# One set of transposes for the value and the one-hot columns of the gate, and the table's products one slot later

## The chip, the cores and the metric

The kernel runs on one core of a Trainium2 chip, in one launch. The metric is the device time in microseconds (us) from the start to the end of one execution. Engines: PE is TensorE (matrix products and transposes), PEld its weight loads, DVE VectorE, ACT ScalarE, POOL GpSimd, SP SyncE, which issues most DMAs.

## The reference

Causal attention over 8 batches of 12 heads, 448 tokens each, and behind it a mixture of 8 experts that takes at most 80 tokens per expert, the 80 with the largest gate weight over all 3584 tokens. In short:

```python
scores = where(causal, q @ k.T / 8, -1e9);  attn = softmax(scores);  x = attn @ v     # 8 x 12 x 448 x 64
logits = x @ w_gate;  e = argmax(logits);  p = softmax(logits)[e]                      # 3584 tokens, 8 experts
for each expert e: tok = tokens of e, at most capacity = 80, those with the largest p
    out[tok] = p[tok] * (relu(x[tok] @ w1[e]) @ w2[e])                                 # other rows are 0
```

## The kernel before

**Attention.** Heads are worked two at a time, 6 pairs to a batch, 48 pairs. A pair takes 8 slots. In slots 0 to 6 PE makes a tile of scores `sp` (L423, L424, the last one L433 to L436) from float16 halves of q and k (`qk`), DVE adds the mask, scales and takes the minimum (`ns`, L445), and ACT takes the exponent (`prob`, L448). In slots 0, 2, 4 and 6 PE also transposes four blocks of the pair before (`tp`, L465), which ACT copies to `PT` (L477). In slot 7 the products with v follow (`xp`, L495), which DVE copies out (L500). Two pairs are one "third" of a batch: while one third is worked, the next one's q and k are split in high and low halves, by casts (POOL L384 twice, DVE L387 twice) and subtractions (POOL L390, L391, L395).

**The gate.** When a batch's attention is done, its gate weights, the choice of an expert for each token and the rank of each token within its expert are worked out in the slots of the two batches that follow. `goh` is the one-hot of the chosen expert, `gow` the same times the gate weight `ggw`. `columns` (L698) and `parts` (L709) write with POOL, per 128 tokens, five groups of 8 columns to `mv` (two for the token's place, L703 and L705, three bfloat16 parts of the weight, L713 to L716) and three copies of the one-hot to `oh` (L702). `expert_rows(i)` (L723) turns them by PE: four transposes of `oh` (i=0) and four of the last three groups of `mv` (i=1) into a bank `selt` each (L731), of which DVE copies 24 rows to `ex[:, 0]` and `ex[:, 1]` (L734). With `ex` PE then makes the comparisons: `rl` (L761, the batch against the table of the 80 best so far), `rn` (L745, the batch against itself), which DVE reduces (`lt` L767, `less` L748); `cp` (L774) and `ro` (L779) give the table's new ranks.

**The table.** Some 30 slots later `rr` (L849, two halves) is the one-hot of the tokens' ranks, and `tn` (L859: 8 products with the old table `tab`, absent in the first batch; L862: 4 products with `mv`) gathers the 80 best in PSUM. DVE copies them to `tab` (L873), PE turns that (`rp`, L877) and DVE copies `row` (L881), which the next batch's `rl` needs.

**What sets the order.** It is written out by hand. The tables `STEPS` (batches 0 to 5) and `EARLY` (batch 6) give each step a slot counted from the end of its batch; in a slot the steps stand behind the slot's score group, in slot 6 of a pair between its transposes and the last score group. The last batch has a list of its own (`TAIL`). Each engine works its instructions in the order in which they are written. A step of slot 80 of one batch meets slot 32 of the next, both in the fifth pair of a batch. Small PSUM banks (`selt`, `rl`, `rn`, `cp`, `tn`, `rp`, `gt`, `rt`) share two buffers in turn.

In the sections below, "the third gate" is that of the third batch; it is worked, with the second batch's table, in the fourth batch's fifth pair, which starts at 150.46 us of the trace. The code:

Of the kernel before, what the change touches and what calls it, by code (L numbers as in the profile page):

```python
# [10 lines left out]
BF16 = mybir.dt.bfloat16  # L11
# [6 lines left out]
P = 128  # L18
# [34 lines left out]
def attention_then_moe(  # L53
# [19 lines left out]
    NT = (S + P - 1) // P  # L73
# [24 lines left out]
    def bank(shape, dtype, name):  # L98
        return (ps_x or ps_m).tile(shape, dtype, name=name, tag="x" if ps_x else "misc")
# [20 lines left out]
    NV = 5  # L120
# [11 lines left out]
    for r in range(2):  # L132
        t = akeep.tile([P, OFF_L + NT * P], F32, name=f"prob{r}")
# [7 lines left out]
    for r in range(2):  # L141
        t = akeep.tile([P, NT, PH * P], F32, name=f"vt{r}")
# [74 lines left out]
    mv = one_hots = mv_flat = oh_flat = expert_cols = tables = table_rows = None  # L217
    identb = before = dec = number = number_after = pnum = tbase = wgd = slots_e = slots_t = None
# [32 lines left out]
    def late_constants():  # L251


        def padded(shape, name):
            t = spool.tile(shape, BF16, name=name, tag=name, bufs=1)
            nc.gpsimd.memset(t, 0.0)
            return t
# [21 lines left out]
        def slots():  # L279
            nonlocal mv_flat, mv, slots_e, slots_t  # L280
            many = max(1, NSL)
            slots_e = const.tile([SL, many, E, SL], COUNT, name="slots_e")
            slots_t = const.tile([P, many, NT, SL], COUNT, name="slots_t")
            for t, k in ((slots_e, E), (slots_t, NT)):
                nc.gpsimd.iota(t, [[SL, many], [0, k], [1, SL]], base=0, channel_multiplier=0,
                               allow_small_or_imprecise_dtypes=True)
            mv_flat = padded([P, (NT - 1) * NV * E + 2 * E + P], "mv")
            mv = mv_flat[:, 0:NT * NV * E].rearrange("k (t v e) -> k t v e", v=NV, e=E)

        def operands():  # L290
            nonlocal oh_flat, one_hots, expert_cols, tables, table_rows
# [399 lines left out]
    def select_groups(bt):  # L691

        b = bt.b
        last = b == B - 1
# [147 lines left out]
        def move(s):  # L842
# [43 lines left out]
            if not last and NSL == 1:  # L886
# [549 lines left out]
```

## Time and profile before

| | |
|---|---|
| median of 3 runs | 467.88 us (467.48 to 468.62) |
| profiled execution | 467.61 us |
| its span in the trace | 465.7 us |
| PE busy over the span | 441.2 us (95%) |
| PEld, DVE, ACT, POOL busy | 346.3 (74%), 414.5 (89%), 392.3 (84%), 309.1 (66%) us |
| granted PE clock | 1.00 |

The span is what the trace shows from the first instruction to the last; the execution's own time is 1.9 us more. Busy shares are averages over attention (to about 318 us) and the experts behind it. A row of a timeline gives start, duration, engine, line and operation, out<-in, the tile's shape and a count; instructions of one kind in a row are drawn together. A bracket at its end is idle time of the engine just before, with what ended it. PE works several instructions at once, so its rows overlap; the distance of starts is what an instruction costs PE.

### The profile page before, as it was taken

What the parts mean: (1) busy time and instruction counts of PE and PEld (TensorE: products, weight loads), DVE (VectorE), ACT (ScalarE), POOL (GpSimd) and SP (SyncE); (2) the same over time, 40 slices, a digit from 0 to 9 for tenths busy, and PEclk for the clock granted to TensorE, in tenths of its full rate; (3) what the DMA queues carried; (4) which work ended last, traced back from release to release, by engine and by line L of the source; (5) the groups of instructions that cost most, each with busy time, mean ns of one, the idle gap of its engine ahead of it and who ended that gap; (6) DMA issues with size and microseconds to landing.
All of it is one profiled execution on the core that took longest, in us unless ns stands there. A gap on an engine that the chain in (4) does not pass through costs nothing.

```text
span 465.7 us, 14169 instructions
## 1 busy us (share of the span) xinstructions
PE 441.2 (95%) x4973; PEld 346.3 (74%) x4973; DVE 414.5 (89%) x1286; ACT 392.3 (84%) x1077; POOL 309.1 (66%) x382
## 2 busy tenths in 40 slices
PE   4998999999999999999999999999989999999994
PEld 1676666866777786677777767776558999999993
DVE  6888889988998999899899989989589999999792
ACT  6997989878988997898889789888587998988791
POOL 7999999988987987898798789760153133310001
PEclk9999999999999999999999999999999999999999
DMA  8658899989769578966957987439948999999931
GB/s 217 182 158 236 230 304 275 271 242 306 206 209 297 171 232 253 270 184 211 298 163 223 279 243 220 161 129 344 410 157 274 397 391 391 398 425 423 423 132 44
DMA packets 42998, 120.84 MB, mean 260 GB/s; under 512 B 6146, under 2 KB 23810, under 8 KB 39472
## 3 DMA queue, kind: packets, MB, share of 16 engines
q1 hardware_dynamic: 41712, 116.21, 76.8%
q0 software_dynamic: 1056, 3.51, 2.4%
q8 instruction: 39, 0.64, 0.6%
q10 hardware_dynamic: 160, 0.23, 0.2%
q14 instruction: 31, 0.25, 0.2%
HBM read 96.36 MB, written 23.99 MB: 258 GB/s over the span
## 4 chain that ended last, share of the span: by engine, by line
PE 75%; DVE 9%; POOL 5%; DMA 4%; issue 3%; ACT 2%; SPq 1%; POOLq 0%; DVEq 0%; ACTq 0%
PE xp L495 15%; PE tp L465 15%; PE sp L423 6%; PE sp L424 5%; PE rt L592 4%; PE hp L1231 3%; PE op L1231 3%; PE op L1239 3%; PE sp L433 3%; PE gp L545 3%; PE hp L1246 3%; PE hp L1245 3%; PE hp L1243 2%; DMA qk<-k_t 2%; DVE wl L1165 2%
## 5 line engine op out<-in xcount | busy, mean ns | idle before, releaser
L448 ACT ACTIVATE prob<-ns,nb 128x128 f32<-128x128 f32 (+3 forms) x336 | 177.1, 529 | 23.0 <-DVE nb L445 20.6
L445 DVE CUSTOM_DVE_ANT_0 ns<-sp,mask 128x384 f32<-128x384 f32 (+2 forms) x288 | 116.2, 413 | 20.2 <-PE sp L424 16.5
L465 PE MATMUL tp<-ident,prob 128*128 128x128 f32 x768 | 118.4, 277 | 1.1 <-ACT prob L448 0.9
L477 ACT COPY PT<-tp 128x512 f32<-128x512 f32 x182 | 104.1, 573 | 17.8 <-PE sp L423 8.4
L395 POOL TENSOR_TENSOR qk<-qk,qk 128x448 f16<-128x448 f32 x92 | 95.8, 1063 | 13.1 <-DVE qk L387 7.4
L465 PEld LDWEIGHTS tp<-ident,prob 128*128 128x128 f32 x768 | 89.8, 142 | 12.1 <-ACT PT L477 2.5
L1165 DVE SCALAR_TENSOR_TENSOR wl<-wraw,wh 128x768 f16<-128x768 f32 (+1 forms) x91 | 92.5, 1081 | 3.2 <-ACT wh L1180 3.2
L495 PE MATMUL xp<-PT,vt 128*64 128x448 f32 (+3 forms) x768 | 91.1, 380 | 0.0
L495 PEld LDWEIGHTS xp<-PT,vt 128*64 128x64 f32 x768 | 53.8, 137 | 42.7 <-issue 22.7
L423 PE MATMUL sp<-qk 128*128 128x384 f16 (+2 forms) x288 | 75.9, 279 | 8.2 <-ACT qk L355 5.2
L1180 ACT ACTIVATE wh<-wraw 128x768 f16<-128x768 f32 (+1 forms) x91 | 79.0, 931 | 3.6 <-PE hp L1246 1.8
L424 PE MATMUL sp<-qk 128*128 128x384 f16 (+2 forms) x288 | 78.3, 278 | 1.3 <-DVE qk L349 0.8
L448 ACT ACTIVATION_READ_ACCUMULATOR prob<-ns,nb 128x1 f32 x336 | 64.0, 190 | 0.0
L1332 POOL DMA_INDIRECT out<-yo,idx x8 | 14.7, 1832 | 70.8 <-ACT yo L1329 66.6
L390 POOL TENSOR_TENSOR qk<-qk,qk 64x448 f16<-64x448 f32 x46 | 54.8, 1190 | 3.4
L391 POOL TENSOR_TENSOR qk<-qk,qk 64x448 f16<-64x448 f32 x46 | 51.0, 1109 | 3.2
L423 PEld LDWEIGHTS <-qk 128*128 128x128 f16 x288 | 28.5, 99 | 17.3 <-issue 8.0
L387 DVE CAST qk<-qk 128x896 f16<-128x896 f32 x46 | 40.4, 879 | 0.1
L384 POOL CAST qk<-qk 64x896 f16<-64x896 f32 x40 | 37.4, 935 | 4.4 <-PE sp L436 3.2
L1246 PEld LDWEIGHTS <-wl 128*128 128x128 f16 x362 | 36.1, 100 | 0.9 <-DVE wl L1165 0.7
L1243 PEld LDWEIGHTS <-wh 128*128 128x128 f16 x362 | 36.4, 101 | 0.0
L1245 PEld LDWEIGHTS <-wh 128*128 128x128 f16 x362 | 36.2, 100 | 0.0
(192 smaller groups left out, 927.7 us busy)
## 6 DMA issues: line engine op xcount, KB each, us to landing
wraw<-w SPq DMA_DIRECT2D x27, 1536.0 KB, 15.7
qk<-k_t SPq DMA_DIRECT2D x92, 224.0 KB, 5.5
out<-mask_l SPq DMA_DIRECT2D x56, 192.0 KB, 4.6
qk<-q_t SPq DMA_DIRECT2D x23, 448.0 KB, 4.2
vt<-v_t SPq DMA_DIRECT2D x24, 384.0 KB, 5.7
xs<-xr SPq DMA_DIRECT2D x42, 192.0 KB, 2.9
wraw<-w SPq DMA_DIRECT2D x24, 256.0 KB, 5.9
vt<-v_t SPq DMA_DIRECT2D x24, 64.0 KB, 5.3
```

What stands on the lines that cost most here:

```text
L390: nc.gpsimd.tensor_tensor(out=qa[hi, i], in0=qf[lo, i], in1=qa[lo, i], op=ALU.subtract)
L391: nc.gpsimd.tensor_tensor(out=qb[lo, i], in0=qf[hi, i], in1=qb[hi, i], op=ALU.subtract)
L395: nc.gpsimd.tensor_tensor(out=k_lo[j][:, i], in0=kf[j][:, i], in1=k_hi[j][:, i], op=ALU.subtract)
L423: nc.tensor.matmul(sp[:, 0:w], qx[:, p, t * P:w], kx[:, p, 0:w], start=True, stop=False)
L424: nc.tensor.matmul(sp[:, 0:w], qx[:, p, t * P:w], lx[:, p, 0:w], start=False, stop=True)
L445: pr.masked = nc.vector.tensor_tensor_reduce(out=ns[:, 0:w], in0=sp[:, 0:w], in1=m, scale=-1.0 / 8.0, scalar=HUGE, op0=ALU.add, op1=ALU.mi ...
L448: nc.scalar.activation(pr.P[:, off:off + w], ns[:, 0:w], AF.Exp, bias=nb, scale=-1.0, accum_out=total)
L465: nc.tensor.transpose(pr.tp[:, i], pr.P[:, off:off + P], ident)
L477: copy(dst, src)
L495: state["pe"] = nc.tensor.matmul(xp[rows, 0:w], st["vt"][:, c, p * P + j * DH:p * P + (j + 1) * DH], pr.PT[:, j, n0:n0 + w], start=(c == 0 ...
L1165: return nc.vector.scalar_tensor_tensor(out=l, in0=src, scalar=SW, in1=h, op0=ALU.mult, op1=ALU.subtract)
L1180: nc.scalar.activation(h, src, AF.Copy, scale=SW)
```

## The change

For the first seven batches the one-hot copies move into `mv`. Per 128 tokens `mv` gets 16 groups of 8 columns (128 columns) in place of 5; the values stand in groups 2 to 6, the three one-hot copies in groups 8 to 10, the rest stays zero from the one memset at the start, which grows from 264 to 544 columns. One set of four transposes (`both_rows`) turns all of it into one bank; the two copies take rows 64 to 87 (`ex[:, 0]`) and rows 32 to 55 (`ex[:, 1]`) of that bank. The last batch keeps its two sets, with its copies by ACT. 28 transposes, their 28 weight loads and seven banks go. In the tables, `parts` goes from slot 33 to 32, the transposes stand in slot 33 (before: 32 and 34), the copies in 34 and 35, and `tn`, `tab`, `rp` and `row` go from 77, 78, 80, 81 to 78, 79, 81, 82. In `EARLY` only the transposes and copies move.

```diff
-STEPS = {... 'parts': 33, 'r0t': 32, 'r0c': 33, 'r1t': 34, 'r1c': 35, 'rl': 36, ... 'rr': 73, 'tn': 77, 'tab': 78, 'rp': 80, 'row': 81, 'rr_more': 75}
-EARLY = {... 'parts': 32, 'r0t': 33, 'r0c': 33, 'r1t': 34, 'r1c': 34, 'rl': 35, ...}
+STEPS = {... 'parts': 32, 'r1t': 33, 'r0c': 34, 'rl': 36, 'lt': 36, 'r1c': 35, ... 'rr': 73, 'tn': 78, 'tab': 79, 'rp': 81, 'row': 82, 'rr_more': 75}
+EARLY = {... 'parts': 32, 'r1t': 33, 'r0c': 34, 'r1c': 35, 'rl': 35, ...}
...
-            mv_flat = padded([P, (NT - 1) * NV * E + 2 * E + P], "mv")
-            mv = mv_flat[:, 0:NT * NV * E].rearrange("k (t v e) -> k t v e", v=NV, e=E)
+            mv_flat = padded([P, NT * P + 4 * E], "mv")
+            mv = mv_flat[:, 0:NT * P].rearrange("k (t v e) -> k t v e", t=NT, e=E)
...
-            m, oh3 = bt.m, bt.oh3 = mv, one_hots
+            m = bt.m = mv[:, :, 2:2 + NV, :]
+            oh3 = bt.oh3 = one_hots if last else mv[:, :, 8:11, :]
...
-                (nc.scalar.copy if last else nc.vector.tensor_copy)(bt.ex[0:3 * E, i], got[0][0:3 * E])
+                nc.scalar.copy(bt.ex[0:3 * E, i], got[0][0:3 * E])
             return [turn, copy]
+
+        def both_rows():
+            got = []
+
+            def turn():
+                selt = bank([P, NT * P], BF16, "selt")
+                got.append(selt)
+                for t in range(NT):
+                    nc.tensor.transpose(selt[:, t * P:(t + 1) * P], mv_flat[:, t * P:(t + 1) * P], identb)
+
+            def copy(i):
+                r = 4 * E if i else 8 * E
+                nc.vector.tensor_copy(bt.ex[0:3 * E, i], got[0][r:r + 3 * E])
+            return [turn, lambda: copy(0), lambda: copy(1)]
...
-        r0, r1 = expert_rows(0), expert_rows(1)
+        rows = [f for i in range(2) for f in expert_rows(i)] if last else both_rows()
```

Three places show the new order. On PE, at the first batch's table (from the second batch on, eight more `tn` products with `tab` stand ahead of these four), before:

```order
L424 MATMUL sp<-qk_1_115 128x384
L862 LDWEIGHTS rr
L862 MATMUL tn<-mv,rr 80x40
L862 LDWEIGHTS rr
L862 MATMUL tn<-mv,rr 80x40
L862 LDWEIGHTS rr [waits DVE_49]
L862 MATMUL tn<-mv,rr 80x40
L862 LDWEIGHTS rr
L862 MATMUL tn<-mv,rr 80x40
L465 MATMUL tp<-ident,prob_104 128x128 [waits Activation_49]
L465 MATMUL tp<-ident,prob_104 128x128 x3
L433 LDWEIGHTS qk_1_115
```

and now (L862 of before is L877):

```order
L424 MATMUL sp<-qk_1_115 128x384
L465 MATMUL tp<-ident,prob_104 128x128 [waits Activation_49]
L465 MATMUL tp<-ident,prob_104 128x128 x3
L877 LDWEIGHTS rr
L877 MATMUL tn<-mv,rr 80x40
L877 LDWEIGHTS rr
L877 MATMUL tn<-mv,rr 80x40
L877 LDWEIGHTS rr [waits DVE_49]
L877 MATMUL tn<-mv,rr 80x40
L877 LDWEIGHTS rr
L877 MATMUL tn<-mv,rr 80x40
L433 LDWEIGHTS qk_1_115
```

The fourth group of attention transposes has moved ahead of the table's products.

On PE, around the transposes of the third gate, before the second set stands behind a group of attention transposes:

```order
L465 MATMUL tp<-ident,prob_106 128x128 [waits Activation_49]
L465 MATMUL tp<-ident,prob_106 128x128 x3
L731 LDWEIGHTS mv [waits DVE_49,Pool_49]
L731 MATMUL selt<-identb,mv 128x128 [waits PE_49]
L731 LDWEIGHTS mv
```

and now the only set stands one score group earlier than that, behind the second score tile of the pair and the turned table `rp`:

```order
L424 LDWEIGHTS qk_1_115
L424 MATMUL sp<-qk_1_115 128x128 [waits Pool_49]
L892 LDWEIGHTS tab_1_680 [waits DVE_49]
L892 MATMUL rp_2761<-identb,tab_1_680 128x80
L745 LDWEIGHTS mv [waits Pool_49]
L745 MATMUL selt<-identb,mv 128x128 [waits PE_49]
```

The first set, which stood ahead of that score tile, is gone.

On DVE, in the fifth pair of a batch from its second score tile on (`ns` 128x128 to 128x384 are the masks of its tiles, CAST the two casts of the next third's k), before:

```order
L445 ISA ns,nb<-sp,mask 128x128 [waits PE_49,Activation_49]
L445 ISA nb 128x1
L881 COPY row_0_682<-rp_1977 24x80
L734 COPY ex<-selt 24x512
L387 CAST qk_1_115<-qk_113 128x896 [waits DMAHW1_49,DMAHW0_49]
L445 ISA ns,nb<-sp,mask 128x256 [waits PE_49,Activation_49]
L445 ISA nb 128x1
L445 ISA ns,nb<-sp,mask 128x256 [waits PE_49,Activation_49]
L445 ISA nb 128x1
L734 COPY ex<-selt 24x512
L387 CAST qk_1_115<-qk_113 128x896 [waits DMAHW3_49,DMAHW2_49]
L445 ISA ns,nb<-sp,mask 128x384 [waits PE_49,Activation_49]
```

and now:

```order
L445 ISA ns,nb<-sp,mask 128x128 [waits PE_49,Activation_49]
L445 ISA nb 128x1
L387 CAST qk_1_115<-qk_113 128x896 [waits DMAHW1_49,DMAHW0_49]
L445 ISA ns,nb<-sp,mask 128x256 [waits PE_49,Activation_49]
L445 ISA nb 128x1
L896 COPY row_0_682<-rp_1984 24x80
L749 COPY ex<-selt 24x512
L445 ISA ns,nb<-sp,mask 128x256 [waits PE_49,Activation_49]
L445 ISA nb 128x1
L749 COPY ex<-selt 24x512
L387 CAST qk_1_115<-qk_113 128x896 [waits DMAHW3_49,DMAHW2_49]
L445 ISA ns,nb<-sp,mask 128x384 [waits PE_49,Activation_49]
```

The `row` copy and the first `ex` copy have moved behind the first cast and one mask; the cast stands where they stood. The order on POOL and SP is the same as before.

## Rows read from the trace of the kernel before

**Rows 1.** Busy time of the engines in a stretch of one batch's length: start:end, length, then busy us (instructions) of PE, PEld, DVE, ACT and POOL, the granted PE clock, DMA share, GB/s.

```profile
143.97:184.33 40.36, 39.92 (x372) 29.27 (x372) 37.59 (x143) 35.31 (x113) 34.61 (x44) 1.00 0.78 230
```

**Rows 2.** All waits of PE from 66 to 310 us, the six batches in which the gates run: what waited for what, us in total, times, longest.

```profile
PE tn L862 <- DVE rr L849: 1.9, 5, 0.6
PE tp L465 <- ACT prob L448: 0.5, 1, 0.5
PE rt L592 <- DVE gfm L652: 0.3, 1, 0.3
PE sp L423 <- DVE nb L445: 0.3, 1, 0.3
```

**Rows 3.** PE's timeline around the second batch's table products, a pair ahead of the third gate's transposes.

```profile
146.71 0.45 PE L859 MATMUL tn<-tab,rm 80*80 80x5 bf16 x8
147.01 0.23 PE L862 MATMUL tn<-mv,rr 128*80 128x40 bf16 x2
147.57 0.25 PE L862 MATMUL tn<-mv,rr 128*80 128x40 bf16 x2 [0.32 <-DVE rr L849]
147.66 0.64 PE L465 MATMUL tp<-ident,prob 128*128 128x128 f32 x4
148.23 0.38 PE L433 MATMUL sp<-qk 128*64 128x448 f16 x1
```

**Rows 4.** DVE's timeline at the same place.

```profile
147.20 0.32 DVE L849 TENSOR_TENSOR rr<-rank,slots_t 128x160 bf16<-128x160 f16 x1
```

**Rows 5.** ACT's timeline at the same place: the copy that empties the bank which the fourth group of attention transposes takes.

```profile
145.99 0.57 ACT L477 COPY PT<-tp 128x512 f32<-128x512 f32 x1
```

**Rows 6.** PE's timeline around the two sets of transposes of the third gate.

```profile
151.06 0.39 PE L731 MATMUL selt<-identb,oh 128*128 128x128 bf16 x4
...
151.62 0.60 PE L465 MATMUL tp<-ident,prob 128*128 128x128 f32 x4
152.25 0.38 PE L731 MATMUL selt<-identb,mv 128*128 128x128 bf16 x4
152.47 0.27 PE L423 MATMUL sp<-qk 128*128 128x256 f16 x1
```

**Rows 7.** DVE's timeline in the same pair.

```profile
151.93 0.18 DVE L881 COPY row<-rp 24x80 bf16<-24x80 bf16 x1
152.04 0.40 DVE L734 COPY ex<-selt 24x512 bf16<-24x512 bf16 x1
152.37 0.60 DVE L387 CAST qk<-qk 128x896 f16<-128x896 f32 x1
...
153.59 0.41 DVE L734 COPY ex<-selt 24x512 bf16<-24x512 bf16 x1
153.92 0.60 DVE L387 CAST qk<-qk 128x896 f16<-128x896 f32 x1
154.45 0.54 DVE L445 CUSTOM_DVE_ANT_0 ns<-sp,mask 128x384 f32<-128x384 f32 x1
```

**Rows 8.** POOL's timeline in the same pair: the second cast of q and the first subtraction.

```profile
151.39 0.93 POOL L384 CAST qk<-qk 64x896 f16<-64x896 f32 x1
152.40 1.48 POOL L390 TENSOR_TENSOR qk<-qk,qk 64x448 f16<-64x448 f32 x1
```

**Rows 9.** DVE's timeline in the second batch: one of its casts beside POOL's cast of the next rows.

```profile
59.91 1.34 DVE L387 CAST qk<-qk 128x896 f16<-128x896 f32 x1
```

**Rows 10.** POOL's timeline there.

```profile
59.83 0.93 POOL L384 CAST qk<-qk 64x896 f16<-64x896 f32 x1
```

**Rows 11.** DVE's timeline in the first gate's pair: the second cast, beside POOL's subtraction of the next rows.

```profile
73.62 0.60 DVE L387 CAST qk<-qk 128x896 f16<-128x896 f32 x1
```

**Rows 12.** POOL's timeline there.

```profile
73.54 1.58 POOL L390 TENSOR_TENSOR qk<-qk,qk 64x448 f16<-64x448 f32 x1
```

**Rows 13.** POOL's timeline at a place where no cast of DVE meets the subtraction.

```profile
78.42 1.03 POOL L390 TENSOR_TENSOR qk<-qk,qk 64x448 f16<-64x448 f32 x1
```

**Rows 14.** DVE's timeline in the pair behind the third gate's: what empties the two small PSUM banks.

```profile
156.84 0.73 DVE L748 SCALAR_TENSOR_TENSOR less<-rn,ggw,before 128x512 bf16<-128x512 f32 x1
...
158.46 0.21 DVE L779 TENSOR_SCALAR ro<-cp,pnum 80x8 f16<-80x8 f32 x1
```

**Rows 15.** PE's timeline there: the comparison that takes the bank which `ro` empties.

```profile
158.75 0.27 PE L745 MATMUL rn<-ex 128*128 128x256 bf16 x1
```

**Rows 16.** PE's timeline in the first gate's pair: the first set of transposes, the score tile behind the second set, the one behind that, and the first comparison.

```profile
70.44 0.39 PE L731 MATMUL selt<-identb,oh 128*128 128x128 bf16 x4
...
71.66 0.27 PE L423 MATMUL sp<-qk 128*128 128x256 f16 x1
...
73.07 0.32 PE L423 MATMUL sp<-qk 128*128 128x384 f16 x1 [0.27 <-DVE nb L445]
...
73.83 0.38 PE L745 MATMUL rn<-ex 128*128 128x512 bf16 x1
```

**Rows 17.** POOL's timeline there: the last write to `mv` ahead of the transposes.

```profile
71.08 0.24 POOL L716 TENSOR_TENSOR mv<-grest,mv 128x32 bf16<-128x32 f32 x1
```

**Rows 18.** PE's timeline in the last batch's attention, behind the table products of the sixth batch: transposes of rows (`rt`), and the last score group.

```profile
309.87 0.52 PE L592 MATMUL rt<-ident,xu 128*128 128x128 f32 x3 [0.31 <-DVE gfm L652]
...
310.76 0.38 PE L433 MATMUL sp<-qk 128*64 128x448 f16 x1
```

**Rows 19.** The memset of `mv` in the view of its line: duration in ns, start in us, shape.

```profile
L256 POOL MEMSET mv<- x1: 309/309/309, 36.9 to 36.9; 128x264 bf16 x1
```

More of the change, by code (lines that the diff above doesn't have):

```diff
@@ L32 @@
 ROWS1 = [59, 62, 64, 65]
-STEPS = {'gp': 18, 'gs': 18, 'lp': 21, 'lg': 22, 'logit': 23, 'shifted': 25, 'chosen': 26, 'sums': 27, 'one_hot': 28, 'weight': 28, 'weighted': 31, 'columns': 30, 'parts': 33, 'r0t': 32, 'r0c': 33, 'r1t': 34, 'r1c': 35, 'rl': 36, 'lt': 36, 'c3w': 38, 'c3l': 39, 'cp': 40, 'ro': 41, 'c2w': 41, 'c2l': 43, 'c1w': 43, 'c1l': 44, 'c0w': 46, 'c0l': 46, 'gt': 47, 'earlier': 51, 'own': 47, 'rank': 51, 'places': 63, 'places_more': 66, 'rr': 73, 'tn': 77, 'tab': 78, 'rp': 80, 'row': 81, 'rr_more': 75}
-EARLY = {'gp': 18, 'gs': 18, 'lp': 21, 'lg': 21, 'logit': 22, 'shifted': 24, 'chosen': 26, 'sums': 27, 'one_hot': 28, 'weight': 29, 'weighted': 31, 'columns': 30, 'parts': 32, 'r0t': 33, 'r0c': 33, 'r1t': 34, 'r1c': 34, 'rl': 35, 'lt': 35, 'c3w': 36, 'c3l': 37, 'cp': 38, 'ro': 39, 'c2w': 39, 'c2l': 40, 'c1w': 40, 'c1l': 41, 'c0w': 41, 'c0l': 42, 'places': 43, 'places_more': 43, 'gt': 44, 'earlier': 44, 'own': 44, 'rank': 46, 'rr': 46, 'tn': 48, 'tab': 50, 'rp': 51, 'row': 52, 'rr_more': 46}
+STEPS = {'gp': 18, 'gs': 18, 'lp': 21, 'lg': 22, 'logit': 23, 'shifted': 25, 'chosen': 26, 'sums': 27, 'one_hot': 28, 'weight': 28, 'weighted': 31, 'columns': 30, 'parts': 32, 'r1t': 33, 'r0c': 34, 'rl': 36, 'lt': 36, 'r1c': 35, 'c3w': 38, 'c3l': 39, 'cp': 40, 'ro': 41, 'c2w': 41, 'c2l': 43, 'c1w': 43, 'c1l': 44, 'c0w': 46, 'c0l': 46, 'gt': 47, 'earlier': 51, 'own': 47, 'rank': 51, 'places': 63, 'places_more': 66, 'rr': 73, 'tn': 78, 'tab': 79, 'rp': 81, 'row': 82, 'rr_more': 75}
+EARLY = {'gp': 18, 'gs': 18, 'lp': 21, 'lg': 21, 'logit': 22, 'shifted': 24, 'chosen': 26, 'sums': 27, 'one_hot': 28, 'weight': 29, 'weighted': 31, 'columns': 30, 'parts': 32, 'r1t': 33, 'r0c': 34, 'r1c': 35, 'rl': 35, 'lt': 35, 'c3w': 36, 'c3l': 37, 'cp': 38, 'ro': 39, 'c2w': 39, 'c2l': 40, 'c1w': 40, 'c1l': 41, 'c0w': 41, 'c0l': 42, 'places': 43, 'places_more': 43, 'gt': 44, 'earlier': 44, 'own': 44, 'rank': 46, 'rr': 46, 'tn': 48, 'tab': 50, 'rp': 51, 'row': 52, 'rr_more': 46}
 ROWS_EARLY = [22, 26, 29, 43]
@@ L729, in turn @@
                 for t in range(NT):
-                    src = mv_flat[:, (t * NV + 2) * E:][:, 0:P] if i else oh_flat[:, t * 3 * E:][:, 0:P]
+                    src = mv_flat[:, t * P + 4 * E:][:, 0:P] if i else oh_flat[:, t * 3 * E:][:, 0:P]
                     nc.tensor.transpose(selt[:, t * P:(t + 1) * P], src, identb)
             def copy():
-                (nc.scalar.copy if last else nc.vector.tensor_copy)(bt.ex[0:3 * E, i], got[0][0:3 * E])
+                nc.scalar.copy(bt.ex[0:3 * E, i], got[0][0:3 * E])
             return [turn, copy]
+        def both_rows():
[9 more added lines that the diff above has]
+            return [turn, lambda: copy(0), lambda: copy(1)]
         def compare(t):
@@ L896, in select_groups @@
         moves = [f for s in range(NSL) for f in move(s)]
-        steps = {"columns": columns, "parts": parts, "r0t": r0[0], "r0c": r0[1], "r1t": r1[0], "r1c": r1[1],
+        steps = {"columns": columns, "parts": parts, **dict(zip(("r0t", "r0c", "r1t", "r1c") if last else ("r1t", "r0c", "r1c"), rows)),
                  "places": places, "places_more": places_more, "earlier": earlier, "own": own, "rank": rank}
```

## The prediction

> **What bounds the kernel now.** I read first the table by stage. In a stretch of one batch PE is busy 39.92 of 40.36 us at granted clock 1.00, DVE 37.59 [rows 1]. So in attention PE sets the pace, and work taken from PE or idle time taken away is worth something only until DVE, with some 2.8 us to spare per batch, is late for PE. Next the waits of PE over the six batches with gates [rows 2]: 3.0 us in all, of which 1.9 are five waits of the table's products for `rr`, one per batch. Then the timelines of PE, DVE and POOL in one batch, since the waits view tells who is last now and not who is next. I take the second batch's table and the third gate as the pattern for five batches (the other four stand at the same distances), and the first gate and the last batch's attention apart.
>
> **The table's products.** PE has issued the first ten of twelve by 147.05 and waits for the second half of `rr` until 147.57 [rows 3]; that half runs on DVE at 147.20 for 0.32, to 147.52 [rows 4]. The fourth group of attention transposes, which stood behind the wait (147.66), now goes ahead of the products. Its bank is free at 145.99 + 0.57 = 146.56 [rows 5], before PE gets there at 146.71, so it doesn't wait. Now `rr` is still there at 147.52, the last two products start at 147.57 and end at 147.82, and the last score group, which starts 0.07 before the end of what stands ahead of it (148.23 against 147.66 + 0.64 = 148.30), starts at 147.75 in place of 148.23: **0.48 per batch**, at that place. The copy `tab`, `rp` and `row` come later, but `rl`, which needs `row`, is over 5 us on.
>
> **The transposes.** A set of four costs PE 0.22 (152.25 to 152.47) [rows 6], and seven sets go: 7 x 0.22 = 1.5 us of PE's work. Whether PE can use it hangs on DVE, since `rl` behind it needs `ex`. That is the part to be worked out.
>
> **DVE's order behind it.** Now DVE does `row` at 151.93, `ex[:, 0]` at 152.04, the first cast at 152.37, then two masks, `ex[:, 1]` at 153.59 and the second cast at 153.92 [rows 7]. `row` and the first `ex` go behind the first cast and one mask. With PE 0.48 earlier, DVE reaches that cast at 151.93 - 0.48 = 151.45. POOL's chain starts from DVE's `goh`, ahead of this, so POOL's second cast of q stays at 151.39 [rows 8]. Now the two casts meet, 0.06 apart. Two meetings of this kind are in the trace. DVE's cast at 59.91, 0.07 to 0.08 behind POOL's cast at 59.83, took 1.34 in place of 0.60, and POOL's took its usual 0.93: it was held until POOL's end at 60.76 and then ended 0.49 later [rows 7, 9, 10]. DVE's cast at 73.62, as far behind POOL's subtraction at 73.54, took 0.60, and the subtraction 1.58 in place of 1.03 [rows 11 to 13]. One of them holds the other; who takes hold first does not follow from the start in the records, which lies ahead of the hold on both engines.
>
> The Trainium skill, page "SBUF — State Buffer", section "Who interferes with whom", has DVE and GpSimd share a pair of ports as an exclusive lock and says "Issue order, not op shape, decides who blocks." That the one fully blocks the other the trace bears out (1.34 against 0.60), that the earlier start wins it does not in the second meeting. By that rule POOL would win here, which is the first rival below.
>
> I take DVE as the winner, by a little: behind 0.07 it lost once and won once, and 0.06 is nearer. Then: first cast 151.45 to 152.05, mask at 151.98, `row` 152.32, `ex[:, 0]` 152.43 to 152.83, mask, `ex[:, 1]` at 153.10, second cast issued at 153.44. POOL's cast is held, ends near 152.85, and the subtraction behind it runs from 152.92 for its own 1.03 [rows 13] to 153.95; DVE's second cast, issued 0.5 behind its start, is held until then and ends 0.49 later, and the next mask starts at 154.36 in place of 154.45 [rows 7]. So DVE is **only 0.09 earlier**, though PE is 0.48 earlier. From there on DVE is the late one. PE waits a little for `rl` (`ex[:, 0]` at 152.83 in place of 152.44), and then for the banks that `less` at 156.84 and `ro` at 158.46 to 158.67 empty [rows 14]; the comparison at 158.75 starts 0.08 behind that [rows 15]. Their chain moves with DVE, by 0.09 to 0.15. I take **0.12 gained per batch**, 5 x 0.12 = 0.6. Both ends: nothing of 0.48 kept, or all.
>
> **The first gate.** There is no table yet, so no wait goes. PE comes to the one set near 70.55 (70.44, where the first set stands, and about 0.1 for the score tile that now goes ahead, an estimate), but the last part of the weight is written by POOL from 71.08 to 71.32 at best [rows 16, 17], and the transposes of the one-hot, which needed only the earlier writes, now wait for it too. That is a new wait of PE of 0.8; if DVE's cast of 0.60, now issued near 71.08 also, takes hold first, POOL's write slips by some 0.5, to 71.85, and PE waits 1.3. From 70.44 to 71.66 PE now needs 1.22; without one set (0.22) and the tile that goes ahead (0.1) it is 0.88, so the tile at 71.66 comes at 72.2 to 72.73, 0.54 to 1.07 later. The idle 0.27 at 73.07 and the gap ahead of it (0.4 from start to start) take 0.4 of that. I take DVE first: 1.07 - 0.41 = **0.66 lost**, the comparison from 73.83 to 74.49; range 0.2 to 0.8.
>
> **The last batch's attention.** There the wait of 0.31 in front of the row transposes goes [rows 18], since they, and the attention transposes, now stand ahead of the products: the score group at 310.76 starts 0.40 earlier. Of this `row`, which comes a slot later with `rl` right behind, gives back some 0.15. **0.25 gained**; range 0 to 0.4.
>
> **What costs nothing.** The memset of `mv` goes from 264 to 544 columns, from 0.31 [rows 19] to at most twice that, at 36.9, where no wait of PE names POOL; if that cover were gone, it would cost 0.3 once. POOL's writes to `mv` have the same shapes. The single bank per gate in place of two can only free a buffer earlier. `ex` is copied from other rows of the bank, with the same shape.
>
> **Sum.** 0.66 - 0.6 - 0.25 = -0.2: the profiled execution goes from 467.61 (span 465.7 and 1.9 around it) to 467.4. The median of the runs shown is 0.27 above that execution, so the forecast is 467.7, with an own range from 466.8 (0.25 per batch kept and 0.3 lost at the first gate) to 468.3 (nothing kept, 0.66 lost, 0.25 gained).
>
> **Rivals.** *Slower: POOL's cast takes hold first* in five batches, as at 59.91. Then DVE's first cast is held to 151.39 + 0.93 = 152.32 and ends 0.49 later, the mask starts at 152.72, `row` and `ex[:, 0]` follow to 153.57, `rl` can start at 153.7, and the second cast is issued at 154.18, inside POOL's second subtraction. That ends near 154.8 (the first from 152.40, held like now, to 153.8, the second 1.03 more), the cast some 0.45 later, and the next mask starts at 155.21 in place of 154.45, 0.76 late. `less`, `ro` and the comparisons follow, and PE, whose 0.48 is long gone, loses some 0.74 per batch: 5 x 0.74 + 0.66 - 0.25 = +4.1, **472.0**. It decides if DVE's cast starts more than 0.06 to 0.07 behind POOL's. For it: a start 0.07 behind lost to the same instruction, and the rule of the lock; against it: the meeting at 73.62. *Faster: neither cast is held* for long, since PE's gain brings the cast clear ahead of POOL's or the second one meets no subtraction; then 0.48 stays in each batch: 0.66 - 2.4 - 0.25 = -2.0, **465.9**. For it: PE bounds and DVE has 2.8 us per batch to spare; against it: 0.06 is on the wrong side, and the second cast comes 0.5 behind the subtraction in any case. *Mixed*: some batches held, some not, 468.5 to 470. That the change does not do what it says is not open: the order shows the sets merged and the products moved.
>
> **Chances.** Forecast 0.51, POOL first 0.25, neither held 0.19, mixed 0.05. About 0.3% (1.4 us) is what a measurement of this kernel can tell from no change. Faster by more than that (under 466.5): nearly all of 0.19 and a little of the forecast, 0.21. Slower (over 469.3): 0.25 and most of the mixed, 0.28. Within: 0.51. The range takes in POOL first, 472.2, and below the forecast a part of the faster case, 466.0; left out are the rest of that and a first gate worse than 0.8.
>
> **What would show it.** In the waits of PE, "tn <- DVE rr" goes down from 1.9 to under 0.5; a new wait of `selt` for POOL's `mv` near 70.6 of 0.8 to 1.3; new waits for `ex`, `less` or `ro`. In the timelines, DVE's first cast in each fifth pair takes 0.60 with POOL's cast near 1.46 (forecast), or near 1.35 with POOL's at 0.93 (slower). The length of one batch, some 40.4 now, is 40.3 by the forecast, 41.1 if POOL is first, 39.9 if neither is held. The prediction is wrong if PE keeps what it gains although DVE is late, that is if `less` and `ro` have more room than I read, or if the two casts start at another distance than 0.06.

## The result and the profile after

The changed kernel took 472.33 us (median of 6 runs, 471.66 to 473.53) beside 467.81 (6 runs): 1.0098 of the time before, interval 1.0087 to 1.0110. That is 4.5 us slower, just outside the range given, at its slow end. The profiled execution took 471.88, its span is 469.8.

The waits of PE after, from 66 to 315 us (what waited for what, us in total, times, longest), beside [rows 2]:

```profile
PE sp L423 <- DVE nb L445: 2.2, 10, 0.3
PE tp L465 <- ACT prob L448: 1.8, 6, 0.5
PE rl L776 <- DVE ex L749: 1.0, 5, 0.2
PE selt L745 <- POOL mv L717: 0.6, 1, 0.6
```

The waits of `tn` for `rr` are gone, and new ones have come: five for `ex`, nine more for masks (`nb`), five more for exponents (which wait for DVE's `nb` in turn), one for `mv`. All but the last lead to DVE being late. Where, is read from the start of the products with v (`xp`, L495) in each pair, in the timelines of PE before and after; one batch is shown, the pairs counted from 0 in a batch:

| pair | 2 | 3 | 4 | 5 | 0 | 1 | 2 |
|---|---|---|---|---|---|---|---|
| before | 142.07 | 148.63 | 155.07 | 161.06 | 167.36 | 174.22 | 182.50 |
| after | 143.28 | 149.37 | 155.77 | 162.25 | 168.92 | 176.08 | 184.36 |
| after less before | 1.21 | 0.74 | 0.70 | 1.19 | 1.56 | 1.86 | 1.86 |
| step | | -0.47 | -0.04 | +0.49 | +0.37 | +0.30 | 0.00 |

(The offset of 1.21 at its start has piled up before.) The other batches have the same steps within 0.02 or 0.03: 0.47 is gained at the table's products, given back in pair 5, and then 0.65 more is lost in the first two pairs of the next batch. Five batches lose 5 x 0.65 = 3.2. The rest is small: +0.24 from the first gate's pair to the next batch's first, -0.04 in the last batch, 0.4 behind attention, and 0.3 ahead of the first gate, where the profiles of kernels that do not differ there lie up to 1.1 apart.

**The gain.** PE's timeline after, at the place of [rows 3]: the products run without a stop.

```profile
148.66 0.37 PE L877 MATMUL tn<-mv,rr 128*80 128x40 bf16 x4
148.97 0.38 PE L433 MATMUL sp<-qk 128*64 128x448 f16 x1
```

**The fifth pair.** DVE's timeline after, at the place of [rows 7] (1.20 is to be added to those):

```profile
152.59 0.62 DVE L387 CAST qk<-qk 128x896 f16<-128x896 f32 x1
...
153.47 0.18 DVE L896 COPY row<-rp 24x80 bf16<-24x80 bf16 x1
153.66 0.42 DVE L749 COPY ex<-selt 24x512 bf16<-24x512 bf16 x1
154.11 0.42 DVE L445 CUSTOM_DVE_ANT_0 ns<-sp,mask 128x256 f32<-128x256 f32 x1
...
154.58 0.41 DVE L749 COPY ex<-selt 24x512 bf16<-24x512 bf16 x1
154.92 0.68 DVE L387 CAST qk<-qk 128x896 f16<-128x896 f32 x1
155.63 0.56 DVE L445 CUSTOM_DVE_ANT_0 ns<-sp,mask 128x384 f32<-128x384 f32 x1
```

And POOL's timeline there, beside [rows 8]:

```profile
152.62 1.38 POOL L384 CAST qk<-qk 64x896 f16<-64x896 f32 x1
154.08 1.04 POOL L390 TENSOR_TENSOR qk<-qk,qk 64x448 f16<-64x448 f32 x1
155.19 1.30 POOL L391 TENSOR_TENSOR qk<-qk,qk 64x448 f16<-64x448 f32 x1
```

DVE's cast started 0.03 ahead of POOL's and was not held (0.62); POOL's was (1.38). But the two `ex` copies do not overlap with their neighbours as before: `row` ends at 153.65 and the copy starts at 153.66, where before the copy started 0.07 ahead of the end; and the masks behind them start late too, the second one with the cast in between (155.63, where the cast ends at 155.60; before, 0.07 ahead of that end). And the second cast is held by the subtraction until 155.12. The mask at 155.63 stands against 154.45 + 1.20 = 155.65: of the 0.48 DVE has 0.02 left.

**The next batch's first pair.** DVE's timeline there, before:

```profile
164.63 0.62 DVE L387 CAST qk<-qk 128x896 f16<-128x896 f32 x1
...
168.56 1.38 DVE L387 CAST qk<-qk 128x896 f16<-128x896 f32 x1
```

POOL's, before:

```profile
164.65 1.50 POOL L390 TENSOR_TENSOR qk<-qk,qk 64x448 f16<-64x448 f32 x1
```

DVE's, after:

```profile
165.83 1.44 DVE L387 CAST qk<-qk 128x896 f16<-128x896 f32 x1
...
170.57 1.37 DVE L387 CAST qk<-qk 128x896 f16<-128x896 f32 x1
```

POOL's, after:

```profile
165.75 1.03 POOL L390 TENSOR_TENSOR qk<-qk,qk 64x448 f16<-64x448 f32 x1
```

Before, the first cast started 0.02 ahead of the subtraction, took 0.62, and the subtraction was held (1.50 for 1.03). After, DVE is where it was (165.83 is 164.63 + 1.20), but POOL is 0.10 earlier (165.75 against 165.85), and now the cast is held: 1.44, that is 0.82 of DVE lost, in each of five batches. POOL is earlier since it was held less in the fifth pair: before, two subtractions by 0.45 and 0.44 (1.48 and 1.47 for 1.03); after, the cast by 0.45 and one subtraction by 0.27.

### The profile page after: what moved, and what is told of

It is laid out like the page before. It is cut to its first block, busy times and chain, and to the rows that moved or that the text cites. A ratio compares the mean times of both kernels' runs of the same rounds, so it can differ in the third digit from the quotient of the medians.

```text
span 469.8 us, 14106 instructions
## 1 busy us (share of the span) xinstructions
PE 441.0 (94%) x4945; PEld 344.6 (73%) x4945; DVE 419.3 (89%) x1286; ACT 391.3 (83%) x1077; POOL 308.1 (66%) x382
## 4 chain that ended last, share of the span: by engine, by line
PE 72%; DVE 13%; issue 5%; DMA 4%; ACT 3%; POOL 2%; SPq 0%; POOLq 0%; DVEq 0%; ACTq 0%
PE xp L495 15%; PE tp L465 13%; PE sp L423 6%; PE sp L424 5%; DMA qk<-k_t 4%; PE rt L592 3%; DVE ns L445 3%; PE hp L1246 3%; PE op L1246 3%; PE gp L545 3%; PE sp L433 3%; PE op L1254 3%; PE hp L1260 2%; PE hp L1261 2%; PE hp L1258 2%
## 5 line engine op out<-in xcount | busy, mean ns | idle before, releaser
L495 PE MATMUL xp<-PT,vt 128*64 128x448 f32 (+3 forms) x768 | 91.1, 380 | 0.0
L495 PEld LDWEIGHTS xp<-PT,vt 128*64 128x64 f32 x768 | 53.8, 137 | 42.7 <-issue 22.6
L1347 POOL DMA_INDIRECT out<-yo,idx x8 | 15.8, 1975 | 69.6 <-ACT yo L1344 65.4
L391 POOL TENSOR_TENSOR qk<-qk,qk 64x448 f16<-64x448 f32 x46 | 51.3, 1116 | 3.2
L390 POOL TENSOR_TENSOR qk<-qk,qk 64x448 f16<-64x448 f32 x46 | 50.0, 1086 | 4.1 <-DVE qk L384 0.7
L387 DVE CAST qk<-qk 128x896 f16<-128x896 f32 x46 | 44.9, 977 | 1.8 <-DMA qk<-k_t 1.8
L384 POOL CAST qk<-qk 64x896 f16<-64x896 f32 x40 | 39.8, 996 | 7.5 <-PE sp L436 6.3
L423 PEld LDWEIGHTS <-qk 128*128 128x128 f16 x288 | 28.5, 99 | 16.6 <-issue 8.0
L424 PEld LDWEIGHTS <-qk 128*128 128x128 f16 x288 | 28.6, 99 | 12.4 <-issue 9.2
L1258 PEld LDWEIGHTS <-wh 128*128 128x128 f16 x362 | 36.4, 101 | 0.0
```

The lines of the kernel that those rows point to most:

```text
L390: nc.gpsimd.tensor_tensor(out=qa[hi, i], in0=qf[lo, i], in1=qa[lo, i], op=ALU.subtract)
L391: nc.gpsimd.tensor_tensor(out=qb[lo, i], in0=qf[hi, i], in1=qb[hi, i], op=ALU.subtract)
L423: nc.tensor.matmul(sp[:, 0:w], qx[:, p, t * P:w], kx[:, p, 0:w], start=True, stop=False)
L424: nc.tensor.matmul(sp[:, 0:w], qx[:, p, t * P:w], lx[:, p, 0:w], start=False, stop=True)
L495: state["pe"] = nc.tensor.matmul(xp[rows, 0:w], st["vt"][:, c, p * P + j * DH:p * P + (j + 1) * DH], pr.PT[:, j, n0:n0 + w], start=(c == 0 ...
```

## The experiments

Theory T: the loss is this hold in the first pair. R: it is the order of the gate's copies behind the cast and the wait of `rl` for them. Diffs are against the kernel after or before, as named. The table has, for each, the measured time with that of the kernel before beside it, and the steps per batch, formed as above from the starts of `xp` against the profile of before, as means over the five batches (the sum takes in pair 2, where only e5c has a step, +0.04). In the first gate, outside these batches, after loses 0.24, e6 0.78, e7 0.94, the others at most 0.28.

| | us | before | ratio (interval) | pair 3 | 4 | 5 | 0 | 1 | sum |
|---|---|---|---|---|---|---|---|---|---|
| after | 472.33 | 467.81 | 1.0098 (1.0087 to 1.0110) | -0.47 | -0.04 | +0.50 | +0.35 | +0.31 | +0.65 |
| e3 | 470.09 | 468.07 | 1.0044 (1.0027 to 1.0061) | -0.47 | -0.04 | +0.50 | +0.33 | +0.25 | +0.57 |
| e4 | 468.19 | 468.07 | 1.0006 (0.9995 to 1.0018) | -0.47 | -0.04 | +0.49 | 0.00 | 0.00 | -0.02 |
| e5 | 468.02 | 468.07 | 1.0004 (0.9979 to 1.0029) | 0.01 | 0.00 | 0.00 | 0.00 | 0.00 | 0.01 |
| e5b | 468.00 | 467.81 | 0.9992 (0.9973 to 1.0010) | 0.00 | 0.00 | 0.00 | 0.00 | 0.00 | 0.00 |
| e5c | 470.85 | 467.17 | 1.0069 (1.0052 to 1.0086) | 0.01 | +0.06 | 0.00 | +0.48 | 0.00 | +0.59 |
| e8 | 468.17 | 467.54 | 1.0019 (1.0007 to 1.0032) | 0.01 | 0.00 | 0.00 | +0.19 | 0.00 | +0.21 |
| e2 | 467.11 | 468.07 | 0.9984 (0.9975 to 0.9994) | -0.48 | +0.34 | +0.07 | 0.00 | 0.00 | -0.07 |
| e1 | 474.54 | 467.81 | 1.0134 (1.0096 to 1.0171) | 0.01 | +0.21 | +0.68 | 0.00 | +0.28 | +1.17 |
| e6 | 468.51 | 467.81 | 1.0010 (0.9988 to 1.0032) | -0.47 | -0.14 | +0.60 | 0.00 | 0.00 | -0.02 |
| v1 | 466.90 | 467.81 | 0.9971 (0.9953 to 0.9988) | -0.47 | +0.10 | +0.21 | 0.00 | 0.00 | -0.15 |
| e7 | 471.93 | 467.17 | 1.0097 (1.0080 to 1.0113) | -0.47 | +0.14 | +0.44 | +0.35 | +0.32 | +0.78 |
| v3 | 464.37 | 467.17 | 0.9940 (0.9925 to 0.9954) | -0.47 | 0.00 | 0.00 | 0.00 | 0.00 | -0.47 |
| v4 | 471.28 | 467.30 | 1.0081 (1.0068 to 1.0095) | -0.48 | -0.19 | +1.22 | 0.00 | +0.29 | +0.84 |

**e3, POOL a little later in the first pair** (against after; `h % HB == 1` are the thirds split in a batch's first two pairs).

```diff
...
             def q_low(i):
+                if h % HB == 1 and h > 3 * HB and i == 0:
+                    nc.gpsimd.memset(scratch, 0.0)
```

> The changed kernel with one small POOL memset (128x80, some 0.16 us) ahead of POOL's first subtraction in the first pair of the fourth to eighth batch. Theory T (the loss is the hold of DVE's cast by that subtraction, which starts 0.08 ahead of the cast after the change and 0.02 behind it before): the subtraction starts behind the cast, the cast goes from 1.44 to 0.62 us, and the 0.65 per batch that PE loses in the two pairs behind it comes back: 472.3 - 5 x 0.65 = 469.1 (468.6 to 469.6). Rival R (the loss is the order of the gate's copies on DVE, row and ex behind the first cast, and the wait of rl; the held cast has room): 472.3 or a little more.

The memset took 0.16 but moved the subtraction by less than 0.1. In one of the five batches the cast came free, in the others not. DVE's cast in a batch of each kind:

```profile
165.03 0.62 DVE L388 CAST qk<-qk 128x896 f16<-128x896 f32 x1
...
205.46 1.50 DVE L388 CAST qk<-qk 128x896 f16<-128x896 f32 x1
```

and POOL's subtractions beside them:

```profile
165.03 1.52 POOL L393 TENSOR_TENSOR qk<-qk,qk 64x448 f16<-64x448 f32 x1
...
205.45 1.03 POOL L393 TENSOR_TENSOR qk<-qk,qk 64x448 f16<-64x448 f32 x1
```

At one and the same start to the hundredth DVE wins, 0.01 later it loses; the batch where it won is the one that lost nothing in pairs 0 and 1 (the others +0.41 and +0.31). The steps give back 0.4 in all, where T had 3.2. The time fell by 2.2, most of it outside these batches (0.8 lies ahead of the first gate, where the two kernels do not differ), so it tells little of T; the mechanism is shown within one run.

**e4, the cast one slot earlier in the first pair** (against after).

```diff
...
+        if h % HB == 1 and h > 3 * HB:
+            at = [0, -1] + THIRD_NEXT[2:]
```

> The changed kernel with that cast one slot earlier, ahead of the pair's second mask on DVE, in the same five batches. T: the cast starts 0.2 earlier, ahead of the subtraction, takes 0.62, and the time is 469.1 (468.6 to 469.8, as the second mask comes 0.5 later). R: 472.3 or more.

POOL's subtraction now starts behind the cast in all five batches and is held in its turn. DVE's timeline, and below it POOL's:

```profile
165.11 0.62 DVE L387 CAST qk<-qk 128x896 f16<-128x896 f32 x1
```

```profile
165.21 1.41 POOL L390 TENSOR_TENSOR qk<-qk,qk 64x448 f16<-64x448 f32 x1
```

The steps in pairs 0 and 1 are 0.00, those ahead are as after: the whole loss against before is gone with this one move. R falls: the order of the copies and the wait for `ex` are still there and cost only what the table's products had gained. The time is 0.9 under T's figure and below its range: the steps give back the 3.2 that T had, the medians differ by 4.1, and where the rest lies the traces do not show.

**e5, e5b, e5c and e8: the hold in the kernel before.** e5 and e5b add a DVE memset ahead of the cast (128x80 and 128x320):

```diff
...
             def k_high(j):
+                if h % HB == 1 and h > 3 * HB and j == 0:
+                    nc.vector.memset(scratch, 0.0)
```

> The kernel before with one small DVE memset (128x80, at most 0.2 us) ahead of that cast in the same five batches, so that the cast starts behind POOL's subtraction. T: the cast is held to about 1.4 us, and 5 x 0.65 = 3.2 us are lost: 471.0 (470 to 471.5). R: at most 5 x 0.2: 467.8 to 468.8. If the memset is too short to change who is first, both give 467.8 to 468.3, and the cast still takes 0.62.

> The kernel before with a longer DVE memset (128x320) ahead of the first cast of a batch's first pair in the same five batches as in e5, about 0.17 us, so that the cast starts clearly behind POOL's subtraction. T: the cast takes 1.3 to 1.45 in place of 0.62 and PE loses 0.65 to 0.8 per batch: 471.0 to 472.0. R: at most 5 x 0.17: 468.9.

Neither made a hold. In e5b the cast started 0.15 behind the subtraction and still took 0.56, while the subtraction (start 164.96) took 1.60: POOL seems to have been kept out ahead of the cast already; why is not shown (the memset itself starts 0.04 behind the subtraction, at 165.00). These two tell nothing of the price. e5c moves the reciprocal of the sums ahead of the cast (`NORMS = [0, 1, 2]`):

> The kernel before with one gate instruction of DVE, the reciprocal of the sums (0.33 us of DVE), moved ahead of the first cast of a batch's first pair, in place of behind it: no instruction added. T: the cast is issued 0.3 behind the start of POOL's subtraction, is held until its end (1.15 to 1.25 in place of 0.62), DVE is 0.6 late and PE some 0.4 in each of five batches: 470.0 (469.2 to 471.0). R (the held cast has room): 467.5 to 468.2.

The time came as T expected, for another reason: the reciprocal found its sums late. DVE's timeline:

```profile
165.51 0.42 DVE L524 RECIPROCAL sums<-sums 128x42 f32<-128x42 f32 x1 [0.47 <-ACT sums L518]
165.84 0.67 DVE L387 CAST qk<-qk 128x896 f16<-128x896 f32 x1
```

The cast was hardly held (0.67). e8 makes the hold without touching DVE: POOL's last addition of the ranks goes behind the subtractions (`'rank': 52` in place of 51).

> The kernel before with POOL's last rank addition (0.28 us of POOL) one slot later, behind the two subtractions of a batch's first pair in place of ahead of them; DVE's order and PE's are those of before. T: the subtraction starts 0.28 earlier, at 164.37 in the frame of before, ahead of the cast at 164.64; the cast is held to 165.4 and takes 1.2 to 1.3 in place of 0.62, DVE is 0.6 late, PE some 0.45 in each of five batches: 470.0 (469.2 to 471.0). R (the hold has room, or comes only with the change): 467.5 to 468.0.

The cast was held in all five batches, by a subtraction that started 0.24 ahead of it. POOL's timeline, and below it DVE's:

```profile
163.87 1.03 POOL L390 TENSOR_TENSOR qk<-qk,qk 64x448 f16<-64x448 f32 x1
```

```profile
164.11 1.27 DVE L387 CAST qk<-qk 128x896 f16<-128x896 f32 x1
...
168.69 0.61 DVE L387 CAST qk<-qk 128x896 f16<-128x896 f32 x1
```

It cost 0.19 per batch in place of the 0.45 expected: the second cast of the stretch, held in before (1.38) and after (1.37), came free here (0.61), so that the 0.65 lost came back 4 us later. The time, 468.17, lies just over R's range and 1.8 under T's figure: T's price for a hold does not carry over to the kernel before. So a hold alone is slower (0.19 per batch), but its price is what all the casts of a stretch lose together, and after the change nothing came back.

**e2, the table's steps alone** (against before): `'tn': 78, 'tab': 79, 'rp': 81, 'row': 82`.

> The kernel before with the table's four steps one slot later and nothing else (both sets of transposes kept, the first ex copy ahead of the cast, row behind it). T: DVE's first cast of the fifth pair starts at 151.78 in the frame of before, is held by POOL's cast until 152.32, and all of DVE behind it is 0.07 to 0.17 earlier; POOL is held as long as before, so the cast in the next batch's first pair keeps ahead of the subtraction: 467.0 to 467.6. R: row behind the cast costs part of the loss: 468.5 to 470.

The gain of 0.47 is there; the first cast (at 151.27) is held by POOL's cast (1.06) and 0.41 is given back. The first pair is as before.

**e1, the merge alone** (against after): `tn`, `tab`, `rp`, `row` back in 77, 78, 80, 81.

> The changed kernel with tn, tab, rp and row in the slots of before: the merge of the transposes alone. T (what counts is who holds the port in the fifth and first pair): the fifth pair's first cast comes at 151.81 in the frame of before, is held by POOL's second cast to 152.32, the second cast at 154.4 is held by POOL's second subtraction to 154.9, DVE is 0.9 late per batch, POOL 0.5 early, and the cast in the next first pair is held as well: about 1.2 per batch on PE, 474 (471 to 475). Rival R2 (a saved set of transposes is a saved 0.22 of PE, and the held cast comes from the later table alone): 467 to 468.

R2 falls. With both sets merged and nothing else the kernel is slower than with both edits. Both casts of the fifth pair and the first one of the next batch are held. DVE's timeline:

```profile
153.07 0.84 DVE L387 CAST qk<-qk 128x896 f16<-128x896 f32 x1
...
155.53 0.86 DVE L387 CAST qk<-qk 128x896 f16<-128x896 f32 x1
...
166.61 1.06 DVE L387 CAST qk<-qk 128x896 f16<-128x896 f32 x1
```

**e6, copies from other rows** (against e4).

```diff
...
-            m = bt.m = mv[:, :, 2:2 + NV, :]
-            oh3 = bt.oh3 = one_hots if last else mv[:, :, 8:11, :]
+            m = bt.m = mv[:, :, 10:10 + NV, :]
+            oh3 = bt.oh3 = one_hots if last else mv[:, :, 0:3, :]
...
-                r = 4 * E if i else 8 * E
+                r = 12 * E if i else 0
```

> The changed kernel with the cast of the batch's first pair one slot earlier, as in e4, and with the one-hot copies in groups 0 to 2 and the values in groups 10 to 14, so that the first ex copy reads rows 0 to 23 (as before the change) and the second rows 96 to 119. Theory S (a DVE copy that reads other rows than it writes does not overlap with the instructions around it; 0.07 to 0.1 at each side): the first ex copy again starts 0.07 before the end of row and the next mask 0.07 before its end, some 0.18 saved on DVE per batch, while the second copy keeps its gap; the time stays at e4's 468.2 (467.7 to 468.4), since the second cast waits for the end of POOL's subtraction all the same. Rival (the gaps come from waits for other engines): the gaps stay. Second rival (DVE's sum alone counts): 468.2 - 5 x 0.18 = 467.3.

DVE's timeline:

```profile
152.38 0.18 DVE L896 COPY row<-rp 24x80 bf16<-24x80 bf16 x1
152.50 0.40 DVE L749 COPY ex<-selt 24x512 bf16<-24x512 bf16 x1
152.83 0.40 DVE L445 CUSTOM_DVE_ANT_0 ns<-sp,mask 128x256 f32<-128x256 f32 x1
153.16 0.07 DVE L445 DVE_READ_ACCUMULATOR2_ANT nb<- 128x1 f32 x1
153.27 0.43 DVE L749 COPY ex<-selt 24x512 bf16<-24x512 bf16 x1
```

The copy from row 0 overlaps again (it starts 0.06 ahead of the end of `row`, the next mask 0.07 ahead of its end), the one from row 96 starts behind the end of the reading ahead of it (153.23). So the gaps belong to the moved rows. The steps of the five batches did not follow: the second cast (at 153.62) was held longer instead (0.90). The time, 468.51, is 0.1 above the range: in the first gate, outside these batches, DVE's cast and POOL's last write to `mv` started level (70.45), the cast went first, the write took 0.72 in place of 0.25 and PE waited 1.1 for it.

**v1, the table alone with `row` in its old place** (against before): `'tn': 78, 'tab': 79`.

> The kernel before with tn and tab one slot later, rp and row where they were, both sets of transposes kept. T: as e2, with row and the first ex copy both ahead of the cast that is held by POOL's second cast of q; the second cast comes 0.11 earlier than in e2, behind a copy, and holds the subtraction; DVE 0.18 earlier than before in each batch, the cast in the first pair keeps ahead: 466.6 (466.2 to 467.1). R (order of the gate's copies unchanged, so nothing of 0.48 is lost): 465.7.

0.15 of the 0.47 is kept in each batch. **e7, the merge with v1's order and e6's layout** (the transposes in slot 32, the copies in 33 and 35):

> The merge of the transposes with the order of v1 kept: transposes in slot 32, the copies in 33 and 35, row in 81, tn and tab in 78 and 79, and the layout of e6 (first copy from row 0, second from row 96). T (DVE bounds here, so PE's 0.22 per set has no taker, and the second copy costs DVE 0.1): v1's time plus 0.1 per batch and 0.2 to 1 for the first gate, whose transposes wait for POOL: 467.5 (467.0 to 468.2). R2 (0.22 of PE saved per gate): 466.9 - 7 x 0.22 = 465.4.

Both missed. The second copy's lost overlap put DVE some 0.2 later than in v1 in the fifth pair, and in the next batch's first pair the cast at 166.28 met a subtraction that started at 166.19: held again, 1.43, and the two steps of after (+0.35, +0.32) are back; another 0.94 went in the first gate, where T had 0.2 to 1. The hold is that of T, and I had not followed it to that pair. In the fifth pair the second cast was free although it started 0.12 behind POOL's subtraction; 11 us later, in the next batch's first pair, it started 0.09 behind and was held. DVE's timeline, and below it POOL's:

```profile
155.09 0.43 DVE L749 COPY ex<-selt 24x512 bf16<-24x512 bf16 x1
155.44 0.60 DVE L387 CAST qk<-qk 128x896 f16<-128x896 f32 x1
...
166.28 1.43 DVE L387 CAST qk<-qk 128x896 f16<-128x896 f32 x1
```

```profile
155.32 1.63 POOL L391 TENSOR_TENSOR qk<-qk,qk 64x448 f16<-64x448 f32 x1
...
166.19 1.03 POOL L390 TENSOR_TENSOR qk<-qk,qk 64x448 f16<-64x448 f32 x1
```

**v3, v1 with the fifth pair's casts moved away from POOL** (against before, `tn` and `tab` as in v1):

```diff
...
+        if h % HB == 0 and h > 2 * HB:
+            at = [0, 1, 3] + THIRD[3:]
```

> v1 with the two casts of the fifth pair placed where POOL is about to finish: the first behind the pair's third mask, the second behind the fifth mask and lt, in the same five batches. T (DVE bounds through the hold of its casts): the first cast is held 0.1 in place of 0.33, the second 0.1 to 0.2, and DVE keeps 0.35 to 0.4 of the 0.48 per batch: 465.7 (465.3 to 466.3). R (the casts' place is of no weight): 466.9, as v1.

All of the 0.47 is kept, in five batches and the last: 464.37, 0.9940 of before, the fastest of all; 1.3 better than I expected, since I had taken holds of 0.1 to 0.2 and none of DVE's casts was held. DVE's timeline:

```profile
151.22 0.61 DVE L387 CAST qk<-qk 128x896 f16<-128x896 f32 x1
151.76 0.41 DVE L445 CUSTOM_DVE_ANT_0 ns<-sp,mask 128x256 f32<-128x256 f32 x1
...
152.10 0.41 DVE L734 COPY ex<-selt 24x512 bf16<-24x512 bf16 x1
152.43 0.54 DVE L445 CUSTOM_DVE_ANT_0 ns<-sp,mask 128x384 f32<-128x384 f32 x1
...
153.79 0.61 DVE L387 CAST qk<-qk 128x896 f16<-128x896 f32 x1
```

**v4, v3 with the merge** (e6's layout; in the first gate the transposes two slots later):

> v3 with the merge of the transposes: the order of v3, the layout of e6, and in the first gate the transposes two slots later, behind POOL's last write. What the merge alone brings when the casts are out of POOL's way. T: PE has no waits left in v3, so a set less saves 0.22 in each of five to six gates as long as DVE keeps up; but with PE earlier the two casts are issued 0.2 earlier against POOL and held 0.1 to 0.3 more, and the second copy costs 0.1: between all of it given back and all kept, 463.8 (463.0 to 464.7). R2 (PE alone counts): 462.9.

Outside both, 7.5 us slower than T gave. DVE's timeline, and below it POOL's:

```profile
154.36 0.41 DVE L445 CUSTOM_DVE_ANT_0 ns<-sp,mask 128x256 f32<-128x256 f32 x1
...
154.81 0.43 DVE L749 COPY ex<-selt 24x512 bf16<-24x512 bf16 x1
155.26 0.56 DVE L445 CUSTOM_DVE_ANT_0 ns<-sp,mask 128x384 f32<-128x384 f32 x1
...
156.63 1.40 DVE L387 CAST qk<-qk 128x896 f16<-128x896 f32 x1
```

```profile
156.51 1.03 POOL L395 TENSOR_TENSOR qk<-qk,qk 128x448 f16<-128x448 f32 x1
```

PE saves its 0.19 in pair 4. But from mask to mask around the copy DVE takes 0.90, where v3 takes 0.67, and the second cast, which in v3 started 0.13 ahead of POOL's next subtraction, now starts 0.12 behind it (156.51) and is held: +1.22 in pair 5.

## Why the prediction was wrong

- **The table's products**: right. 0.48 forecast, 0.46 to 0.48 measured, with the wait gone as described.
- **The transposes**: right in size (0.22; 0.19 in v4) and in that PE has no use for it while DVE is late.
- **The meeting in the fifth pair**: right in the outcome, not in its ground. I put DVE's cast 0.06 behind POOL's; it was 0.03 ahead. That DVE won was luck: at 0.06 behind POOL's cast it would have lost, as in e5c's second batch (59.44, 0.06 behind, 1.36). The two meetings I had [rows 9 to 12] differ in what stands ahead of the cast, a mask in the lost one and an `ex` copy in the won one, and the fifteen traces bear that out. Of the casts behind a mask (or a reading of `lt`) that start from 0.1 ahead to 0.3 behind a cast or subtraction of POOL, from 27 us on, all 48 up to 0.005 behind are free and all 115 from 0.013 on are held. Behind an `ex` copy, which starts 0.33 ahead of its cast, all 79 casts up to 0.23 behind are free, and all 35 from 0.34 on are held: there POOL won only where it started ahead of the copy. (An example of the last, in the first gate's pair of the kernel before: a copy at 71.31, its cast at 71.64 with 1.03, POOL's cast at 71.27.) So the change also took the fifth pair's first cast from behind a copy, where it had 0.33 in hand, to behind a mask, where it has none. No run puts a copy ahead of a cast, or takes one away, and changes nothing else.
- **"DVE is only 0.09 earlier"**: 0.02. The term left out the lost overlap around the two copies, four times some 0.1 per batch; I had written that `ex` is copied from other rows "with the same shape" under what costs nothing. Three of the four stand ahead of the second cast, which waits for POOL anyway: e6 takes two of them away and the sum of the steps stays as in e4. The fourth, the mask behind that cast, which starts 0.03 behind its end in place of 0.07 ahead, loses 0.10, more than the 0.07 that is missing.
- **The step that failed**: the working followed the casts in the fifth pair and stopped there, with "their chain moves with DVE". The same five batches have a third meeting 12 us on, in the next batch's first pair, 0.02 wide (164.63 against 164.65). I had no row for it. A change in how long POOL is held in the fifth pair shifts it: by 0.10, and 0.82 of DVE went in each batch. In place of "0.12 gained per batch" the runs show 0.65 lost per batch, 3.2 in all, while the fifth pair itself comes out even (-0.47, -0.04, +0.50); e4 removes exactly that. The slower rival named the mechanism, a held cast, for a place where it did not happen; that its price (0.74 per batch, 472.0) lies near what was measured is chance.
- **The first gate**: 0.66 forecast, 0.16 measured in that pair (0.24 up to the next batch). PE waited 0.6, not 1.3: the cast started 0.04 behind the last write to `mv` and did not delay it. Where it does delay it, as in e6, 0.78 goes, near what I forecast: the size was right for the case that I took, and the case was the other one. **The last batch**: 0.25 gained forecast, 0.04 measured: the 0.40 was there, and `row` and `rl` took 0.36 back, not 0.15.
- **A slip in the sum**: the lower end of the forecast's own range comes to 466.7 from its terms, not 466.8.

The Trainium skill's rule that issue order decides who blocks ("SBUF — State Buffer", "Who interferes with whom") agrees with every cast behind a mask here (ahead by 0.02 or level: free; behind by 0.01 or more: held). It does not with the cast's own start in the records where a copy or a memset stands ahead of it (0.12 behind in e7, 0.15 in e5b: free).

What stays open: whether the merge can be kept at a gain. v4 shows that PE saves 0.19 per gate by it, and that it is paid for on DVE, by a copy without overlap; no run has it with all casts free. Open too is why a memset ahead of a cast helps it (e5, e5b).

## What to carry to other kernels

Where two engines hold each other off for a whole instruction, list every place where their instructions start within a tenth of a microsecond, over a full period of the schedule, before moving anything: a shift of 0.1 was worth 0.8 of DVE here, and it need not be where the edit is. Placing the two engines' long instructions apart (v3) was worth more than the work removed (e1, e7, v4). A step that is taken off the busiest engine gains nothing while the next engine is late in the same stretch.

## What the runs showed of the hardware

- A DVE cast of 0.62 behind a mask goes first if it starts level with POOL's cast or subtraction and waits for its end if it starts 0.01 later (e3: 0.62 and 1.50; so it is in all 163 such meetings in the fifteen traces). Behind an `ex` copy the start of the copy, 0.33 ahead of the cast, decides as far as the rows show (114 meetings; the last free one 0.23 behind POOL's start, the first held one 0.34). Not every instruction ahead does that: behind a product of 0.55 (`xr`) the casts are held from 0.11 behind POOL's start on (1.41). The loser takes some 0.45 (POOL) to 0.9 (DVE) longer where the two start nearly together.
- A DVE copy that reads rows 64, 32 or 96 of a PSUM bank, behind an instruction that read row 0 on, starts 0.01 to 0.03 behind the end of the one ahead in place of 0.07 ahead of it, and so does the next mask, which reads row 0 on again, directly behind the copy or with a cast in between (after, e7, v4). The cast in between, which reads no PSUM, overlaps as ever, and so does a copy from row 0 at both sides (e6).
